# Attention and a gated convolution FFN on one core: P as the stationary operand, row sums from a column of ones, and an order of work written out

## The chip, the cores and the metric

The kernel runs on one core of one Trainium2 chip. The metric is the device time in microseconds (us). The kernel before has a median of 295.88 us over three runs (295.88 to 300.52).

## The reference

The core of what is computed, for 8 batches of 8 heads, 576 positions and 64 columns a head, in float32:

```python
scores = scale * np.matmul(q, k.transpose(0, 1, 3, 2))
cum = np.cumsum(np.log(np.clip(f, 0.0001, 1.0)), axis=-1)
decay = cum[:, :, :, None] - cum[:, :, None, :]
scores = np.where(causal, -1000000000.0, scores + decay)
attn = np.exp(scores - np.max(scores, axis=-1, keepdims=True))
attn = attn / (np.sum(attn, axis=-1, keepdims=True) + 1e-09)
x = np.matmul(attn, v)               # then heads side by side: 576 x 512 a batch
h = np.maximum(x @ w_in, 0.0)        # 576 x 1024
conv_out = sum(conv_w[k] * hp[:, k:k + S, :] for k in range(3))   # over positions, hp is h padded
out = (h * 1.0 / (1.0 + np.exp(-conv_out))) @ w_out
```

## The kernel before

Every batch has an attention part and an FFN part. Four heads make a group, `hb`, so there are 16 groups, two for each batch; two heads of a group are a pair, `i`.

Loading. `load_qk` (L199) fetches q and k of a group with transposing DMAs, seen as 16-bit halves of the float32 values: 128 rows, of which the odd ones hold the upper halves. The even rows carry the decay: `clamp` (L205, on VectorE) overwrites them for the first six groups, and `rows_of` (L220, L221) or, from the seventh group on, `fill` (L214, L215) bring constants and the cumulated logarithms from two images in DRAM, which `constants` and L289 to L291 write at the start. The first group adds the decay with two more matmuls (L323, L325). V comes in by `load_v` (L228, five DMAs a batch) and is cast to fp16 on GpSimd (`cast_v`, L234 and L236). Four q and k tiles go round.

Attention. The scores stand transposed: keys in partitions, queries along the columns (L320). `off_scores` does the blocks off the diagonal of one head in 1024 columns, `diag_scores` the four diagonal blocks of two heads, `tail_scores` the last 64 positions of four heads. ScalarE takes the exponentials from PSUM (L347, L357, L332). Diagonal and tail go through a float32 tile to GpSimd, which masks them (`diag_mask` L360, `tail_mask` L335). P then streams through TensorE twice (`sweep`, L381): `sums` with columns of ones as weights, the four pairs of a batch into one PSUM tile, and `pv` with V as weights, so that x comes out transposed. `recip` turns the sums round (L391) and inverts them (L392), `spread` spreads them over 64 partitions (L395), and `norm` multiplies (L404) into `xt`.

FFN. `ffn1` (L414) multiplies a 128-row tile of w_in with xt; `relu` (L418, ScalarE) halves the result; `conv` (L424, L426, VectorE) does the three taps; `tanh` (L429, ScalarE) and `gate` (L433, VectorE) make the gated value; `ffn2` (L440, L445, in the last batch L454, L457) multiplies with w_out; `evac` (L465, L467) copies from PSUM and `store` (L473, L476) writes. The weights come through GpSimd's DMA queue, which casts them (L500).

Order. `Plan.add` takes each piece of work with its engines, an estimated time, what it waits for, and a priority. `Plan.play` runs a list schedule over these when the program is built and emits the pieces in that order; at run time each engine follows its own queue in order. Four PSUM tiles of 1024 float32 columns (`ps`) are shared by all, with further limits (`sc`, `mm`, `pv`) on how many of them scores, ffn1 and P V may hold.

Of the kernel before, what the change touches and what calls it, by code (L numbers as in the profile page):

```python
# [9 lines left out]
FP32 = mybir.dt.float32  # L10
# [7 lines left out]

class Plan:


    ENGINES = ("PE", "ACT", "DVE", "POOL", "SP")

    def __init__(self, rooms):
        self.tasks = []
        self.rooms = rooms
        self.slot = {}

    def add(self, engines, after, key, fn, take=(), give=(), lag=0.2, dma=0.0, behind=()):
        after = [a for a in after if a is not None]  # L30
        behind = [a for a in behind if a is not None]
        self.tasks.append(dict(engines=engines, after=after, behind=behind, key=key, fn=fn, take=list(take),
                               give=list(give), lag=lag, dma=dma))
        return len(self.tasks) - 1

    def play(self, busy, dma_at, dma_ahead):
        tasks, rooms = self.tasks, self.rooms
        left = [len(t["after"]) + len(t["behind"]) for t in tasks]
        due, nxt = [[] for _ in tasks], [[] for _ in tasks]
        for k, t in enumerate(tasks):  # L40
            for a in t["after"]:
                due[a].append(k)
            for a in t["behind"]:
                nxt[a].append(k)
        free = {r: [(0.0, j) for j in range(n)] for r, n in rooms.items()}
        ready = {e: [] for e in self.ENGINES}
        busy = dict(busy)
        heap, order, started = [], [], set()
        dma_free, now = dma_at, 0.0

        def open_(k):
            for e in tasks[k]["engines"]:
                heapq.heappush(ready[e], (tasks[k]["key"], k))

        for k in range(len(tasks)):
            if not left[k]:
                open_(k)
        for e in self.ENGINES:
            heapq.heappush(heap, (busy[e], -1, ""))
        while len(started) < len(tasks):  # L60
            if not heap:
                raise RuntimeError("the plan is stuck")
            now = heap[0][0]
            while heap and heap[0][0] <= now:
                _, k, what = heapq.heappop(heap)
                if what == "give":
                    for r, taker in tasks[k]["give"]:
                        free[r].append((now, self.slot[taker, r]))
                elif what == "done":
                    for d in due[k]:  # L70
                        left[d] -= 1
                        if not left[d]:
                            open_(d)
            for e in self.ENGINES:
                if busy[e] > now:
                    continue
                kept = []
                while ready[e]:
                    key, k = heapq.heappop(ready[e])
                    if k in started:  # L80
                        continue
                    t = tasks[k]
                    if any(not free[r] for r in t["take"]):
                        kept.append((key, k))
                        continue
                    if t["dma"] and dma_free > now + dma_ahead:
                        kept.append((key, k))
                        heapq.heappush(heap, (dma_free - dma_ahead, -1, ""))
                        continue
                    for r in t["take"]:  # L90
                        free[r].sort()
                        self.slot[k, r] = free[r].pop(0)[1]
                    started.add(k)
                    for d in nxt[k]:
                        left[d] -= 1
                        if not left[d]:
                            open_(d)
                    order.append((now, k, e))
                    end = now + t["engines"][e]
                    busy[e] = end  # L100
                    heapq.heappush(heap, (end, -1, ""))
                    if t["dma"]:
                        dma_free = max(dma_free, now) + t["dma"]
                        end = max(end, dma_free)
                    if t["give"]:
                        heapq.heappush(heap, (end + 0.1, k, "give"))
                    heapq.heappush(heap, (end + t["lag"], k, "done"))
                    break
                for x in kept:
                    heapq.heappush(ready[e], x)  # L110
        return order, now
# [3 lines left out]
def kernel(  # L115
# [15 lines left out]
    NKB = 5  # L131
# [10 lines left out]
    RING, NP, NPT, NVA, NVF, NHT, NU, NOB = 4, 6, 4, 4, 2, 4, 3, 3  # L142
    NCL = 6
    AB = 256
# [4 lines left out]
    dpool = ctx.enter_context(tc.tile_pool(name="dram", bufs=1, space=bass.MemoryType.DRAM))  # L149
    psum = ctx.enter_context(tc.tile_pool(name="psum", bufs=1, space=bass.MemoryType.PSUM))  # L150

    image = dpool.tile([4, 2, BH, S], BF16, name="image")
    blank = dpool.tile([60, 2 * HS], BF16, name="blank")
    ident = cpool.tile([128, 128], FP32, name="ident")
# [4 lines left out]
    cwrow = cpool.tile([3, D_FF], FP32, name="cwrow")  # L159
    kc = cpool.tile([128, S], BF16, name="kc")  # L160
    one1 = cpool.tile([128, 1], FP32, name="one1")
    lim = cpool.tile([128, 4], FP32, name="lim")
    lit = cpool.tile([128, 5], FP32, name="lit")
    lii = cpool.tile([128, 3], I32, name="lii")
    hix = cpool.tile([128, 4], I32, name="hix")
    hfx = cpool.tile([128, 4], FP32, name="hfx")
    sel_k = cpool.tile([128, 4], BF16, name="sel_k")
    sel_q = cpool.tile([128, 4, 128], BF16, name="sel_q")
    ones_h = cpool.tile([128, 4, 64], FP16, name="ones_h")
# [4 lines left out]
    vf_t = [cpool.tile([128, H, NKB, 64], FP32, name=f"vf{t}") for t in range(NVF)]  # L174
    va_t = [cpool.tile([128, HH, NKB, 64], FP16, name=f"va{t}") for t in range(NVA)]
    pp_t = [cpool.tile([128, 3072], FP16, name=f"pp{t}") for t in range(NP)]
    pt_t = [cpool.tile([128, HH * SL], FP16, name=f"pt{t}") for t in range(NPT)]
    pd_t = [cpool.tile([128, 1024], FP32, name=f"pd{t}") for t in range(2)]
    p3_t = [cpool.tile([128, HH * SL], FP32, name=f"p3{t}") for t in range(2)]
    st_t = [cpool.tile([128, S], FP32, name=f"st{t}") for t in range(1)]  # L180
    rt_t = [cpool.tile([128, 18, 4], FP32, name=f"rt{t}") for t in range(2)]
    rb_t = [cpool.tile([128, S], FP32, name=f"rb{t}") for t in range(2)]
    xt_t = [cpool.tile([128, NCC, S], FP16, name=f"xt{t}") for t in range(2)]
    ht_t = [cpool.tile([128, S + 2], FP16, name=f"ht{t}") for t in range(NHT)]
    u_t = [cpool.tile([128, S], FP32, name=f"u{t}") for t in range(NU)]
    hg_t = [cpool.tile([128, NFF, S], FP16, name=f"hg{t}") for t in range(2)]
# [3 lines left out]
    fsb, cum = rb_t[0], rb_t[1]  # L190

    plan = Plan({"ps": 4, "sc": 2, "mm": 2, "pv": 2, "p": NP, "pt": NPT, "pd": 2, "p3": 2, "st": 1, "rt": 2, "rb": 2, "xt": 2, "ht": NHT,
                 "u": NU, "hg": 2, "ob": NOB, "va": NVA, "vf": NVF, "qk": RING})
    slot = plan.slot

# [7 lines left out]
    def clamp(hb, p, side, eng):  # L203
        t = (stq_t, stk_t)[side][hb % RING].bitcast(U16)[:, 2 * p * S:2 * (p + 1) * S]
        eng.tensor_scalar(t, t, lim[:, 2 * side:2 * side + 1], lim[:, 2 * side + 1:2 * side + 2],  # L205
                          op0=ALU.mult, op1=ALU.add)

    def even_rows(hb, first, n, c0, c1):
        t, width = qk_t[hb % RING], 2 * HS + 64
        return bass.AP(tensor=t.tensor, offset=int(t.offset) + first * width + c0, ap=[[2 * width, n], [1, c1 - c0]])  # L210

    def fill(hb):
        c = slice(hb * HH, (hb + 1) * HH)
        nc.sync.dma_start(even_rows(hb, 8, 60, 0, 2 * HS), blank)  # L214
        nc.sync.dma_start(even_rows(hb, 0, 4, 0, 2 * HS).rearrange("j (a x) -> j a x", a=2),  # L215
                          image[:, :, c, :].rearrange("j a h s -> j a (h s)"))

    def rows_of(hb):
        c = slice(hb * HH, (hb + 1) * HH)
        nc.sync.dma_start(even_rows(hb, 0, 1, 0, HS), image[0:1, 0, c, :].rearrange("j h s -> j (h s)"))  # L220
        nc.sync.dma_start(even_rows(hb, 2, 2, HS, 2 * HS), image[1:3, 1, c, :].rearrange("j h s -> j (h s)"))  # L221

    def load_v(b, t_load):
        vf = vf_t[slot[t_load, "vf"]]
        base = int(v.offset) + b * H * S * D
        for kb in range(NKB):
            n = 128 if kb < NKB - 1 else SL
            nc.sync.dma_start(vf[0:n, :, kb, :],  # L228
                              bass.AP(tensor=v.tensor, offset=base + kb * 128 * D, ap=[[D, n], [S * D, H], [1, D]]))
# [465 lines left out]
```

## Time and profile before

The profiled execution has a span of 293.2 us from first to last instruction, on the slowest (and only) core; what lies between it and the median of the runs, 2.7 us, is around the span.

| | busy us | share | instructions |
|---|---|---|---|
| TensorE matmul (PE) | 245.6 | 84% | 2832 |
| TensorE weight load (PEld) | 170.8 | 58% | 2832 |
| VectorE (DVE) | 238.9 | 81% | 322 |
| ScalarE (ACT) | 198.1 | 68% | 266 |
| GpSimd (POOL) | 96.2 | 33% | 133 |

The granted TensorE clock is 0.967 of full speed on average. DMA moves 47.7 MB in 125,683 packets. The first ffn1 matmul (L414) starts at 50.4 us, those of the later batches at 80.4, 114.7, 142.0, 173.2, 202.5, 231.8 and 256.7.

In profile lines, a group reads: line, engine, operation, output<-input, partitions by columns, type, count, busy us and the mean of one in ns. PE is TensorE, DVE VectorE, ACT ScalarE, POOL GpSimd, SP the queue that issues most DMAs. In a timeline the first two numbers are start and length in us. A busy time of PE counts each matmul until its modelled end, so it holds the drain of the pipeline as well as the columns that stream.

### The profile page before, as it was taken

Reading aid. Unit: us, or ns where it says so; the run is one execution under the profiler, and the core shown is the slowest. Engines: PE = TensorE matmul, PEld = TensorE weight load, DVE = VectorE, ACT = ScalarE, POOL = GpSimd, SP = SyncE. Lnnn points to the kernel's source line nnn. Section 1 sums busy time; section 2 is a strip of 40 time slices with the busy share of each in tenths; the row PEclk is TensorE's granted clock in tenths of the full one; section 3 lists DMA queues with packets and bytes.
Section 4 is the critical chain, followed back from the end, with each engine's and each line's share of the span. In section 5 each row is a group of like instructions: output and inputs, shape, how many; then the busy total and the mean of one; then the engine's idle time right before and its main releaser. Section 6 shows DMA issues by size and latency. Waiting matters only on the chain.

```text
span 293.2 us, 6856 instructions
## 1 busy us (share of the span) xinstructions
PE 245.6 (84%) x2832; PEld 170.8 (58%) x2832; DVE 238.9 (81%) x322; ACT 198.1 (68%) x266; POOL 96.2 (33%) x133
## 2 busy tenths in 40 slices
PE   0099539598789799999998999999999999969990
PEld 0078327376655577577755875687568757845630
DVE  4852308979999888997987899889988998899661
ACT  1228626487666998886877878977897798436631
POOL 8625907227340326306256261126112221000000
PEclk9999859979999999999999999999999999979998
DMA  8997999999998999999999999999322002100304
GB/s 164 215 246 127 165 182 188 173 191 191 218 191 127 293 218 169 238 246 268 177 211 227 254 205 198 211 296 178 80 77 80 11 2 104 62 0 32 132 0 162
DMA packets 125683, 47.71 MB, mean 163 GB/s; under 512 B 117470, under 2 KB 120542, under 8 KB 124992
## 3 DMA queue, kind: packets, MB, share of 16 engines
q1 hardware_dynamic: 118852, 43.73, 72.0%
q0 software_dynamic: 6640, 3.25, 8.0%
q8 instruction: 22, 0.36, 0.5%
q10 hardware_dynamic: 160, 0.30, 0.4%
q14 instruction: 9, 0.07, 0.1%
HBM read 19.91 MB, written 10.58 MB: 104 GB/s over the span
## 4 chain that ended last, share of the span: by engine, by line
PE 43%; DVE 24%; ACT 7%; issue 4%; DMA 2%; ACTq 0%; DVEq 0%
PE ps L440 14%; PE ps L414 11%; PE ps L381 8%; DVE u L426 6%; DVE hg L433 5%; PE ps L320 5%; DVE u L424 5%; DVE xt L404 3%; PE ps L454 3%; ACT pp L347 2%; ACT pd L357 2%; DVE rb L395 2%; DMA qk<-image 2%; ACT hg L429 2%; PE ps L445 1%
## 5 line engine op out<-in xcount | busy, mean ns | idle before, releaser
L320 PE MATMUL ps<-qk 128*128 128x128 bf16 (+3 forms) x576 | 63.7, 248 | 30.2 <-DVE qk L205 14.5
L414 PE MATMUL ps<-xt,w_in_f 128*128 128x288 f16 x512 | 74.1, 293 | 4.8 <-DVE xt L404 3.1
L347 ACT ACTIVATE pp<-ps 128x1024 f16<-128x1024 f32 x64 | 64.7, 1027 | 12.2 <-PE ps L320 9.8
L429 ACT ACTIVATE hg<-u,cw 128x576 f16<-128x576 f32 x64 | 49.4, 778 | 24.8 <-DVE u L426 24.5
L320 PEld LDWEIGHTS <-qk 128*128 128x128 bf16 x576 | 39.4, 101 | 42.8 <-issue 15.2
L414 PEld LDWEIGHTS <-w_in_f 128*128 128x128 f16 x512 | 49.9, 100 | 23.9 <-issue 7.3
L360 POOL TENSOR_SCALAR_AFFINE_SELECT pp<-pd 128x1024 f16<-128x1024 f32 x32 | 38.7, 1209 | 73.7 <-ACT pd L357 73.7
L433 DVE SCALAR_TENSOR_TENSOR hg<-hg,ht 128x576 f16<-128x576 f16 x64 | 52.9, 834 | 10.1 <-ACT hg L429 9.9
L424 DVE SCALAR_TENSOR_TENSOR u<-ht,cwt 128x576 f32<-128x576 f16 x64 | 56.4, 894 | 5.9 <-ACT ht L418 5.9
L426 DVE SCALAR_TENSOR_TENSOR u<-ht,cwt,u 128x576 f32<-128x576 f16 x64 | 60.1, 949 | 0.7
L418 ACT ACTIVATE ht<-ps 128x576 f16<-128x576 f32 x64 | 41.4, 657 | 18.9 <-PE ps L414 14.1
L440 PE MATMUL ps<-w_out_f,hg 128*128 128x512 f16 x224 | 51.4, 379 | 2.7 <-ACT pd L357 1.2
L440 PEld LDWEIGHTS <-hg 128*128 128x128 f16 x224 | 21.7, 98 | 26.5 <-issue 2.3
L357 ACT ACTIVATE pd<-ps 128x1024 f32<-128x1024 f32 x32 | 32.8, 1025 | 5.9 <-PE ps L325 2.5
L381 PE MATMUL ps<-pp,ones_h 128*64 128x128 f16 (+3 forms) x576 | 26.3, 242 | 1.5 <-ACT pp L347 0.9
L381 PEld LDWEIGHTS <-ones_h 128*64 128x64 f16 x640 | 23.0, 112 | 6.3 <-issue 4.6
L381 PE MATMUL ps<-pp,va 128*64 128x128 f16 (+3 forms) x576 | 24.8, 239 | 1.7 <-DVE xt L404 1.2
L335 POOL TENSOR_SCALAR_AFFINE_SELECT pt<-p 128x256 f16<-128x256 f32 x16 | 10.3, 641 | 48.7 <-ACT p L332 48.7
L234 POOL CAST va<-vf 128x1024 f16<-128x1024 f32 x16 | 17.8, 1113 | 24.1 <-DMA vf<-in_v_dram 18.1
L381 PEld LDWEIGHTS <-va 128*64 128x64 f16 x640 | 22.4, 110 | 5.6 <-issue 4.1
L395 DVE STREAM_TRANSPOSE rb<-rt 128x576 f32<-128x576 f32 x32 | 22.7, 745 | 0.0
L404 DVE TENSOR_TENSOR xt<-ps,rb 128x576 f16<-128x576 f32 x32 | 22.0, 725 | 0.0
(75 smaller groups left out, 167.6 us busy)
## 6 DMA issues: line engine op xcount, KB each, us to landing
vf<-in_v_dram SPq DMA_DIRECT2D x32, 256.0 KB, 5.6
out_dram<-ob SPq DMA_DIRECT2D x16, 512.0 KB, 2.8
qk<-blank SPq DMA_DIRECT2D x10, 540.0 KB, 5.3
vf<-in_v_dram SPq DMA_DIRECT2D x8, 128.0 KB, 5.1
w_in_f<-in_moe_w_in_dram POOLq DMA_DIRECT2D x4, 256.0 KB, 6.0
w_out_f<-in_moe_w_out_dram POOLq DMA_DIRECT2D x4, 256.0 KB, 7.7
out_dram<-ob SPq DMA_DIRECT2D x16, 64.0 KB, 3.8
blank<-qk POOLq DMA_DIRECT2D x1, 540.0 KB, 4.7
```

What stands on the lines that cost most here:

```text
L320: nc.tensor.matmul(o, tk[:, h * S + k0:h * S + k0 + 128], tq[:, h * S + q0:h * S + q0 + n], start=True, stop=hb > 0)
L347: nc.scalar.activation(pp_t[slot[t_dg, "p"]][:, 1024 * s:1024 * (s + 1)], ps_t[slot[t_sc, "ps"]], AF.Exp, scale=SCALE)
L357: nc.scalar.activation(pd_t[slot[me, "pd"]], ps_t[slot[t_dg, "ps"]], AF.Exp, scale=SCALE)
L360: nc.gpsimd.affine_select(pp_t[slot[t_dg, "p"]][:, 2048:3072].rearrange("p (m j) -> p m j", j=128), pd_t[slot[t_ex, "pd"]].rearrange("p (m ...
L381: nc.tensor.matmul(ps[64 * s:64 * (s + 1), AB + q0:AB + q0 + n], left_of(s, h, m), p, start=first and x in (0, 3), stop=last and x in (2, ...
L414: nc.tensor.matmul(ps[:, MB + 288 * a:MB + 288 * (a + 1)], w_in_f16[:, cc, 128 * ff:128 * (ff + 1)], xt[:, cc, 288 * a:288 * (a + 1)], sta ...
L418: nc.scalar.activation(ht_t[slot[t_m1, "ht"]][:, 1:1 + S], ps_t[slot[t_m1, "ps"]][:, MB:MB + S], AF.Relu, scale=0.5)
L424: nc.vector.scalar_tensor_tensor(u, ht[:, 0:S], cwt[:, ff, 0:1], ht[:, 1:1 + S], op0=ALU.mult, op1=ALU.add)
L426: nc.vector.scalar_tensor_tensor(u, ht[:, 2:2 + S], cwt[:, ff, 1:2], u, op0=ALU.mult, op1=ALU.add)
L429: nc.scalar.activation(hg_t[slot[t_g0, "hg"]][:, ff, :], u_t[slot[t_u, "u"]], AF.Tanh, scale=cw[:, ff, 1:2])
L433: nc.vector.scalar_tensor_tensor(hv, hv, 1.0, ht_t[slot[t_m1, "ht"]][:, 1:1 + S], op0=ALU.add, op1=ALU.mult)
L440: nc.tensor.matmul(o, hg[:, ff, 128 * c:128 * (c + 1)], w_out_f16[:, ff, :], start=(ff == 0), stop=(ff == NFF - 1))
```

## The change

Scores, exponentials, FFN matmuls and their numbers stay. What differs:

- P V: a block of P (128 keys by 128 queries) is the stationary operand, and 65 columns of V move: 64 of a head and one of ones, so that each row sum stands beside its row. x comes out with positions in partitions; `norm` inverts the sums and multiplies, and `turn` transposes x on TensorE into `xt`'s layout, with `turned` copying it on VectorE or ScalarE. `sums`, `recip` and `spread` go.
- Masks of the first eight groups: a matmul puts -1e30 into PSUM above the diagonal before the scores are added, and the exponential goes straight to P in fp16. The other eight groups keep GpSimd's masks.
- Convolution of eight of the 64 tiles (even tiles of batches 0 and 1): three matmuls with diagonal matrices, and tanh reads PSUM.
- Weights: loaded as float32 through SP in eight pieces into the tiles for outputs, and cast by GpSimd, VectorE or ScalarE.
- The two DRAM images go; constants come from an SBUF tile `zc` (`fill`), the rows from `kc`. Clamps serve four groups instead of six, one for each side of a group.
- Order: `play` emits the pieces in the order of the string `ORDER`, which also names the engine of the evacuations, the xt copies and the weight casts. One more `ht` and one more `u` buffer; the limits `sc`, `mm` and `pv` go.

The core of the diff, new functions included:

```diff
+ORDER = """
+q1.1 cl1.1 q3.1 cw q3.0 q2.0 q1.0 cl0.0 sd0 ed0 q2.1 cl0.1 sd1 cl2.0 cwt so0.0 eo0.0 cl1.0 so1.0 eo1.0 v0.0 rw1 ed1
+so0.1 eo0.1 so1.1 eo1.1 v0.3 st0 et0 sd2 so2.1 ed2 so2.0 eo2.0 st1 et1 sd3 so3.1 tw0 ed3 eo3.1 tw2 so3.0 eo3.0 v0.2
+cl2.1 v0.1 rw2 cl3.1 v0.4 va0.0 eo2.1 v1.0 v1.1 va1.0 va1.1 pv0.0 n0.0 va0.1 wi0 cl3.0 sd4 ed4 wi1 wic1@POOL v1.2 sd5
...
+o7.1.2 a7.7 o7.1.3 o7.1.4 o7.1.5 g7.7 o7.1.6 o7.1.7 s5.0 o7.0.4 o7.0.5 o7.0.6 o7.0.7 e6.2@ACT s6.2 o7.2.0 o7.2.1
+o7.2.2 o7.2.3 o7.2.4 o7.2.5 o7.2.6 o7.2.7 e7.1@ACT s7.1 e7.0@ACT s7.0 e7.2@ACT s7.2
+"""
...
+    MASK_PE = (0, 1, 2, 3, 4, 5, 6, 7)
+    CONV_PE = ((0, 0), (0, 2), (0, 4), (0, 6), (1, 0), (1, 2), (1, 4), (1, 6))
...
+    def masked(o, n, j):
+        nc.tensor.matmul(o, ident, mask[:, 0:j].unsqueeze(1).broadcast_to((128, n, j)), start=True, stop=False)
...
+    def pv(hb, u):
+        ps, va = ps_of(f"pv{hb}.{u}"), va_t[slot[f"va{hb}.0", "va"]]
+        for j, n in enumerate(((0, 1), (2, 3), (4,))[u]):
+            for h in range(HH):
+                o = ps[:, 512 * j + (D + 1) * h:512 * j + (D + 1) * (h + 1)]
+                for m in range(n + 1):
+                    nc.tensor.matmul(o, block(hb, h, m, n), va[:, h, m, 0:D + 1], start=(m == 0), stop=(m == n))
+
+    def norm(hb, u):
+        ps, rc, xm = ps_of(f"pv{hb}.{u}"), rc_t[slot[f"n{hb}.{u}", "rc"]], xm_t[slot[f"n{hb}.0", "xm"]]
...
+        nc.vector.reciprocal(r, got[:, :, :, D])
+        nc.vector.tensor_tensor(xm[:, 2 * u:2 * u + nj, :].rearrange("p j (h d) -> p j h d", d=D), got[:, :, :, 0:D],
+                                r.unsqueeze(3).broadcast_to((128, nj, HH, D)), op=ALU.mult)
+
+    def turn(hb):
+        ps, xm = ps_of(f"t{hb}").bitcast(FP16), xm_t[slot[f"n{hb}.0", "xm"]]
+        for n in range(NKB):
+            c = 128 * n if n < 4 else S - 128
+            for cc in range(2):
+                nc.tensor.transpose(ps[:, 1024 * cc + c:1024 * cc + c + 128], xm[:, n, 128 * cc:128 * (cc + 1)], ident)
...
+    def conv_pe(b, ff):
+        ps, ht = ps_of(f"k{b}.{ff}"), ht_of(b, ff)
+        for x in range(3):
+            for a in range(2):
+                nc.tensor.matmul(ps[:, MB + 288 * a:MB + 288 * (a + 1)], taps[:, ff, x, :],
+                                 ht[:, x + 288 * a:x + 288 * (a + 1)], start=(x == 0), stop=(x == 2))
...
+    def fill(hb):
+        for first, n, side in ((0, 63, 0), (2, 62, 1)):
+            src = zc[first:first + n, side:side + 1, :].broadcast_to((n, HH, S))
+            nc.sync.dma_start(even_rows(hb, first, n, side * HS, (side + 1) * HS).rearrange("p (h s) -> p h s", s=S), src)
+
+    def rows_of(hb):
+        c = hb * HH
+        nc.sync.dma_start(even_rows(hb, 63, 1, 0, HS), kc[c:c + HH, :])
+        for j in range(2):
+            nc.sync.dma_start(even_rows(hb, j, 1, HS, 2 * HS), kc[BH * j + c:BH * j + c + HH, :])
```

In `ORDER`, q and k loads are `q<group>.<side>`, V loads `v`, clamps `cl`, rows `rw` and `fi`, scores `sd`, `so`, `st`, their exponentials `ed`, `eo`, `et`, GpSimd's masks `md`, `mt`, P V `pv`, its norm `n`, transposes `t` and `tx`, weights `wi`, `wo` with casts `wic`, `woc`; then ffn1 `f`, relu `r`, convolution `c`, `d` or on TensorE `k`, tanh `a`, gate `g`, ffn2 `o`, evacuation `e`, store `s`.

## The prediction

> **What bounds the kernel now.** I read the page's engine totals first, then the busy time by stretch, then the chain of waits, then groups and timeline for prices.
>
> ```profile
> PE 245.6 (84%) x2832; PEld 170.8 (58%) x2832; DVE 238.9 (81%) x322; ACT 198.1 (68%) x266; POOL 96.2 (33%) x133
> ...
> PE 43%; DVE 24%; ACT 7%; issue 4%; DMA 2%; ACTq 0%; DVEq 0%
> ```
>
> TensorE (PE) and VectorE (DVE) are nearly equal in load, and no engine alone fills the span. So I asked for the busy time by stretch: until the first ffn1 matmul (50.4 us), from there to the first ffn1 matmul of the last batch (256.7), to the end, and for two steady batches in between.
>
> ```profile
> 0.00:50.40 50.40, 27.31 (x349) 21.00 (x349) 23.21 (x46) 21.85 (x24) 28.42 (x63) 0.90 1.02 182
> 50.40:256.70 206.30, 190.64 (x2327) 135.64 (x2325) 190.14 (x243) 160.31 (x219) 67.79 (x71) 0.99 0.87 175
> 256.70:293.20 36.50, 27.66 (x160) 14.19 (x159) 25.56 (x35) 15.94 (x23) 0.00 (x0) 0.93 0.18 65
> ...
> 173.20:202.50 29.30, 28.32 (x345) 20.01 (x345) 27.46 (x36) 24.26 (x34) 9.25 (x11) 1.00 1.07 226
> 202.50:231.80 29.30, 28.33 (x345) 20.03 (x345) 27.47 (x36) 24.26 (x34) 7.42 (x8) 1.00 0.26 76
> ```
>
> Columns after the length are PE, PEld, DVE, ACT, POOL busy, granted clock, DMA share, GB/s. A steady batch takes 29.3 us with PE 28.3 and DVE 27.5 busy: two engines hand the bound to each other. The chain of waits shows the handover, PE work and then the normalisation on DVE alone:
>
> ```profile
> 188.12 0.98 PE ps L414 x8
> 189.09 0.44 PE ps L320 x4
> 189.53 2.21 PE ps L381 x60
> ...
> 194.43 0.70 DVE st L391
> 195.16 0.60 DVE rt L392
> 195.76 1.44 DVE hg L433
> 197.20 0.75 DVE rb L395 x2
> ```
>
> A busy PE is not PE at its pace, since each matmul's span holds its drain. So I price matmuls start to start. The first score stage, after the clock has come up at 21.5 us, has single rows:
>
> ```profile
> 22.01 0.19 PE L320 MATMUL ps<-qk 128*128 128x64 bf16 x1
> 22.04 0.19 PE L323 MATMUL ps<-sel_k,kc 128*128 128x64 bf16 x1
> 22.07 0.19 PE L325 MATMUL ps<-kc,sel_q 128*128 128x64 bf16 x1
> ...
> 22.75 0.22 PE L320 MATMUL ps<-qk 128*128 128x128 bf16 x1
> 22.81 0.22 PE L323 MATMUL ps<-sel_k,kc 128*128 128x128 bf16 x1
> 22.86 0.22 PE L325 MATMUL ps<-kc,sel_q 128*128 128x128 bf16 x1
> ```
>
> 64 columns cost about 29 ns, 128 cost 56, each with a fresh 128x128 weight load in front. From the chain: ffn1 0.98 us per 8 (0.98 x 64 = 62.7), one sweep of L381 2.21/3 = 0.74 (64 sweeps, 47.2), ffn2 7.8 a batch (62.2), scores 2.76 per four heads (44.1, plus 5.5 for the first four heads' extra products). Paced PE work before is 222 us; in 50.4 to 256.7 it is 54.9 + 46.8 + 35.7 + 41.3 = 178.7, or 87% of the 206.3 us; in the two steady batches 54.0 of 58.6, 92%.
>
> **The change, part by part.** On PE: the 64 sweeps go, -47.2. P V becomes 960 pairs of a 128x128 load and a 65-column matmul. No row has 28 such pairs running; the nearest are the 64-column rows, 29 ns, so 30 ns is taken: 28.8. If nothing of the load were hidden, it would be the 100 ns that an LDWEIGHTS of L320 lasts: 96. The low end is 27 ns (the fastest gap of the rows above). 160 transposes at 128 columns: 56 ns, 9.0; between 56 and the same 100 ns load, 16. Mask products of the first eight groups of four heads: 32 of 512 columns at 0.216 (the chain's 1.73 per 8) and 8 of 256, 7.8. Convolution of eight tiles: 48 of 288 columns at 0.1225, 5.9. Net +4.3: PE stays at 226.6, a wash.
>
> The Trainium skill, page "TensorE: Matmul & The Clock Gate", section "Back-to-back issue gap", speaks against this change: it gives about 81 ns for a sustained stream of load-and-matmul pairs at 128 columns. The rows above give 56 ns for such pairs; by the page's figure the 960 pairs would take 78 us and the kernel, as an estimate, some 316.
>
> On DVE: spread, norm, st and rt go (rows L395 22.7, L404 22.0, L391 6.2, L392 4.8), 55.7. Eight of 64 convolutions leave, (56.4 + 60.1)/8 = 14.6. Clamps cover a third fewer elements of 16.1, 5.4. The clip of f (L282), 3.97 us beside POOL's 4.0 us memset of qk (L263), has no such memset now; L286 does a like size in 0.46, so 3.5. Sum removed 79.2. Added: 48 norm products from PSUM. L404 does 576 columns in 0.725 and the 1024-column copy (L467) takes 1.22, so 1.11 ns a column: 32 at 0.65 and 16 at 0.37, 26.7. Reciprocals of 4 or 8 columns, by the 8-column row 0.20: 9.8, by L392's 0.60 at most 28.9. Eight xt copies of 1152 columns, 1.37 each, 10.9; five more large evacuations and a small one 6.5; one weight cast 1.2; masks and identity 0.5. Sum added 55.6. DVE: 215.3 against 238.9. Beyond that, DVE suffers when POOL masks:
>
> ```profile
> 177.02 0.81 DVE L424 SCALAR_TENSOR_TENSOR u<-ht,cwt 128x576 f32<-128x576 f16 x1
> ...
> 178.42 1.64 DVE L426 SCALAR_TENSOR_TENSOR u<-ht,cwt,u 128x576 f32<-128x576 f16 x1
> ...
> 178.22 1.23 POOL L360 TENSOR_SCALAR_AFFINE_SELECT pp<-pd 128x1024 f16<-128x1024 f32 x1 [3.25 <-ACT pd L357]
> ```
>
> Half the POOL masks go; means above 0.81 (0.89 and 0.95, gate 0.83 against 0.75) make 20 us of such loss, so 0 to 10 more off DVE, 6 taken (POOL gets six weight casts of the size of L234, 1.1 us, in exchange). ACT: eight xt copies at 1.1 (between L465's 1.0 and one and an eighth of it), one cast, less five evacuations: 198 + 4.5.
>
> The queues: POOL's 15 DMA issues and the image and blank copies go. SP gets eight weight loads, 24 fills (L214 row 0.88 us) and 45 single rows (L220 0.36), 43 us of issuing in place of 20. The view of SP's waits has it waiting 63 us for evacuations at L473 alone, so this is covered in the steady part. It isn't at the start, where SP issues in order: four half loads until 7 us, six full transposes at 2.65 us each (rows of L199) until 23, the row copies of the second four heads behind their clamp at about 27, landing at 30 (that group's scores started at 27.4 before); while SP stands at them, V's loads wait behind, and POOL's V casts with them. The weight loads follow V at about 33 and are cast by 42, behind ACT's work. What then sets the first ffn1 is ACT's queue: seven exponentials from 16, the rest from 30 on, 15 at about 0.95 (mean 1.03, overlapping by a tenth), so 45 us, with the third and half the fourth group of heads already scored. It was 50.4.
>
> Sum: from first ffn1 to the last batch's, counted in the new order by the same paces, PE has 54.9 ffn1, 45.9 ffn2, 35.1 scores, 25.2 P V, 7.8 transposes, 4.5 masks, 5.8 convolutions, 179.2. DVE's part of this stretch is 215.3 - 6 less some 27 of head and 17 of tail, 165, so 87% of 190 us, where it was 94% in the steady batches. I take a PE efficiency of 94% (steady before 92, whole before 87): 190.6. The tail holds 24.3 us of PE; DVE's eight tiles of 2.14 take 17.1 after 1.6 of ffn1 and relu, then 3.0 of last ffn2, 1.4 evacuation, the 6.3 from the last store's issue to the end, some 2 of earlier gates: 32 against 36.5. 45 + 190.6 + 32 = 267.6, against the profiled 293.2; the median lies 2.7 above that span, so 270.3.
>
> **The rivals.** (1) Every P V pair pays its weight load. For: L381's loads last 110 ns and P is now always the loaded side, 60 pairs per group. Against: the 29 ns rows. At 100 ns the middle grows by 840 x 0.07/0.94 = 62.6 and the head by 4.2: 337 us. It decides from about 63 ns a pair on, where the time passes 302; at 56 ns it is 295, no change.
> (2) The fixed order doesn't meet the real delays: an engine waits at the head of its queue for work that is late while ready work stands behind, and PE stays at its old 87%. For: 33 takes of four PSUM tiles a batch, 30 before. Against: DVE's slack. 179.2/0.866 = 206.9, total 287.
> (3) The start gains nothing, as all loads pass through SP: first ffn1 at 50 to 54. 276 to 279; in the range.
>
> **How the numbers follow.** Forecast with (3) 0.64; better than 258 (98% efficiency, head 43, tail 30) 0.06; rival (2) 0.15, a third of it within 2%; rival (1) 0.15, of which 0.04 ends near 56 ns, within 2%, and 0.11 slower. Faster 0.64 + 0.06 + 0.10 = 0.80, same 0.05 + 0.04 = 0.09, slower 0.11; 2% is about what a measurement of this kernel tells from no change. The range goes from 258 to 288, just past rival (2).
>
> **What would show it.** Right: 65-column matmuls at 30 ns start to start; DVE busy 205 to 215; first ffn1 near 45; 190 us from there to the last batch's. Wrong: those matmuls 60 ns or more apart, a PE idle share as large as before with DVE well below 80%, or SP still issuing first loads when PE stands.

## The result, and the profile after

The changed kernel takes 331.69 us (median of four runs, 328.07 to 332.81), the kernel before, beside it on the same chip, 295.88 us: a ratio of 1.1217, with a 95% interval from 1.1117 to 1.1317. It is slower by 12%, where 270 us had been forecast. The profiled execution has a span of 329.4 us.

First the engine totals, the shares of the chain that ended last (by engine, then by line), and three groups (busy us, mean ns of one, idle before):

```profile
PE 255.7 (78%) x2760; PEld 181.6 (55%) x2760; DVE 207.6 (63%) x327; ACT 203.3 (62%) x269; POOL 70.7 (21%) x109
...
SPq 46%; PE 23%; DMA 20%; POOL 4%; DVE 2%; issue 2%; ACT 2%; ACTq 0%
SPq L195 15%; SPq L215 11%; PE ps L459 10%; DMA qk<-in_q_dram 9%; DMA qk<-kc 7%; SPq L217 7%; SPq L223 5%; PE ps L414 5%; SPq L211 5%; PE ps L308 4%; SPq L477 2%; PE ps L384 2%; DMA ob<-in_moe_w_in_dram 2%; POOL taps L435 2%; DMA vf<-in_v_dram 1%
...
L384 PE MATMUL ps<-va,pp 128*128 128x65 f16 x896 | 36.0, 197 | 0.5 <-ACT pp L349 0.2
...
L391 DVE RECIPROCAL rc<-ps 128x8 f32<-128x8 f32 (+1 forms) x48 | 9.3, 194 | 36.4 <-PE ps L384 35.7
...
L392 DVE TENSOR_TENSOR xm<-ps,rc 128x512 f16<-128x512 f32 (+1 forms) x48 | 28.9, 602 | 1.7
```

The loads of the engines are as forecast: DVE went from 238.9 to 207.6 us. What changed is who ends the wait. Before, PE and DVE held two thirds of the chain and SP none of the lines shown; now SP's issuing (SPq) and transfers (DMA) hold two thirds, 46% and 20%.

Next the busy time by stretch: to the first ffn1 matmul, from there to the last batch's, the tail; then two batches in the middle, a bad one and a good one.

```profile
0.00:46.50 46.50, 29.56 (x353) 22.57 (x354) 21.18 (x53) 21.08 (x23) 15.46 (x47) 0.96 1.00 197
46.50:300.10 253.60, 201.13 (x2235) 144.36 (x2233) 165.94 (x247) 165.03 (x222) 55.20 (x63) 0.91 0.66 146
300.10:329.40 29.30, 24.98 (x177) 14.63 (x175) 20.48 (x29) 17.19 (x26) 0.00 (x0) 0.96 0.34 121
109.00:167.60 58.60, 40.35 (x391) 26.69 (x390) 30.68 (x45) 30.39 (x40) 11.63 (x12) 0.88 0.57 133
167.60:192.90 25.30, 25.30 (x310) 18.53 (x309) 22.48 (x35) 22.88 (x31) 8.02 (x9) 1.00 0.86 190
```

Head 46.5 us (45 forecast) and tail 29.3 (32) are better than before. The middle, 253.6 us where 190.6 had been forecast, holds the whole loss. One of its batches takes 25.3 us with PE busy throughout; in another PE is idle for 31% (40.35 of 58.6) and DVE and ACT for nearly half, with the granted clock down to 0.88.

What PE and its weight loads waited for in the whole run (total us, times, longest), from the view of the waits of each:

```profile
PE ps L308 <- DMA qk<-kc: 42.7, 10, 8.3
...
PEld L308 <- DMA qk<-zc: 30.1, 6, 8.2
```

L308 is the score matmul. It waits for the rows of constants (`zc`) and of cumulated logarithms (`kc`) in q and k. One such wait in the chain (start, length, what):

```profile
78.06 0.70 SPq L211
...
78.81 3.37 SPq L215
...
82.23 1.49 SPq L217
...
83.77 6.49 DMA qk<-kc
90.26 0.09 issue
90.35 0.37 PE ps L308 x4
```

`fill` issues its second piece (L211) in 0.70 us. The next instruction, a copy of one row for each of four heads in one 4.5 KB DMA (L215), then takes 3.37 us to issue, and the first of two more (L217) 1.49; the second, whose issue begins at 83.77 us, lands 6.5 us after that. Only then do the scores of the group start. The view of the transfers for 76 to 91 us shows why, in 40 slices of 0.375 us (busy share of 16 DMA engines in tenths, and rate):

```profile
DMA  9959799765642111111111111111197899995006
GB/s 246 252 120 139 246 377 404 248 190 147 172 144 95 46 37 34 34 37 49 49 43 43 49 49 43 46 37 40 40 180 146 320 389 358 278 133 29 27 18 134
```

For 16 slices, 6 us, the share is a tenth and the rate 34 to 49 GB/s. The packet records of the trace say what runs there. They hold no engine's number, but the packets in flight at a time can be counted: two for the k-side fill, 62 rows of 4 x 1152 bytes, whose 248 packets of about 52 ns each take some 6.4 us; nine for the q-side fill, 63 rows. The kernel before fills a group with 60 rows. In its transfers from 83.5 to 92 us (slices of 0.21 us) the long run of nines is a transpose in 256-byte packets; the fill's 60 packets of 9216 bytes begin only from the thirteenth slice on, at 86.1 us:

```profile
DMA  3199999999309009849459056210000001003899
GB/s 47 35 113 287 290 289 289 290 290 289 63 7 477 0 0 173 304 173 434 173 173 520 0 109 152 65 43 0 0 0 0 0 0 43 0 0 88 204 181 73
```

Of these 60, 15 are in flight at a time from 87 to 88.5 us, and the last ends at 89.3: about 3 us for 540 KB, against 6.4 us for the 62 rows' 279 KB. The Trainium skill, page "DMA: Bandwidth & Descriptors", section "Why a DMA increments its semaphore by 16 and not by 1", has the rule: a copy is spread over the largest number of engines, at most 16, that divides the slowest dimension above 1 of both its sides. The packets in flight agree: 15 for 60 rows, 9 for 63, 2 for 62. Below, packets in flight stand for engines.

The P V matmuls, start to start, at about 41 us (the same columns; xN counts matmuls drawn together):

```profile
40.19 1.56 PE L384 MATMUL ps<-va,pp 128*128 128x65 f16 x44
41.59 0.19 PE L384 MATMUL ps<-va,pt 128*128 128x65 f16 x1
41.62 0.29 PE L384 MATMUL ps<-va,pp 128*128 128x65 f16 x4
41.75 0.19 PE L384 MATMUL ps<-va,pt 128*128 128x65 f16 x1
```

44 take 41.59 - 40.19 = 1.40 us, 32 ns each, with a fresh 128x128 load of P in front of every one.

### The profile page after: what moved, and what is told of

It is laid out like the page before. It is cut to its first block, busy times and chain, and to the rows that moved or that the text cites. A ratio compares the mean times of both kernels' runs of the same rounds, so it can differ in the third digit from the quotient of the medians.

```text
span 329.4 us, 6715 instructions
## 1 busy us (share of the span) xinstructions
PE 255.7 (78%) x2760; PEld 181.6 (55%) x2760; DVE 207.6 (63%) x327; ACT 203.3 (62%) x269; POOL 70.7 (21%) x109
## 4 chain that ended last, share of the span: by engine, by line
SPq 46%; PE 23%; DMA 20%; POOL 4%; DVE 2%; issue 2%; ACT 2%; ACTq 0%
SPq L195 15%; SPq L215 11%; PE ps L459 10%; DMA qk<-in_q_dram 9%; DMA qk<-kc 7%; SPq L217 7%; SPq L223 5%; PE ps L414 5%; SPq L211 5%; PE ps L308 4%; SPq L477 2%; PE ps L384 2%; DMA ob<-in_moe_w_in_dram 2%; POOL taps L435 2%; DMA vf<-in_v_dram 1%
## 5 line engine op out<-in xcount | busy, mean ns | idle before, releaser
L308 PE MATMUL ps<-qk 128*128 128x128 bf16 (+2 forms) x576 | 72.7, 262 | 59.8 <-DMA qk<-kc 42.7
L308 PEld LDWEIGHTS <-qk 128*128 128x128 bf16 x576 | 45.6, 108 | 82.3 <-DMA qk<-zc 30.1
L366 ACT ACTIVATE pp<-ps 128x1024 f16<-128x1024 f32 x64 | 63.8, 1024 | 14.3 <-PE ps L308 11.0
L459 PE MATMUL ps<-w_out_f,hg 128*128 128x512 f16 x256 | 64.5, 402 | 0.8 <-DVE xm L392 0.8
L429 DVE SCALAR_TENSOR_TENSOR u<-ht,cwt 128x576 f32<-128x576 f16 x56 | 46.6, 836 | 10.0 <-ACT ht L424 9.7
L431 DVE SCALAR_TENSOR_TENSOR u<-ht,cwt,u 128x576 f32<-128x576 f16 x56 | 46.2, 836 | 1.3
L384 PE MATMUL ps<-va,pp 128*128 128x65 f16 x896 | 36.0, 197 | 0.5 <-ACT pp L349 0.2
L384 PEld LDWEIGHTS <-pp 128*128 128x128 f16 x896 | 34.3, 100 | 2.5 <-ACT pp L349 0.5
L349 ACT ACTIVATE pp<-ps 128x1024 f16<-128x1024 f32 x16 | 16.3, 1028 | 30.5 <-PE ps L308 19.4
L349 ACT ACTIVATE pd<-ps 128x1024 f32<-128x1024 f32 x16 | 16.3, 1024 | 24.4 <-PE ps L308 24.0
L352 POOL TENSOR_SCALAR_AFFINE_SELECT pp<-pd 128x1024 f16<-128x1024 f32 x16 | 18.4, 1158 | 57.3 <-ACT pd L349 57.3
L392 DVE TENSOR_TENSOR xm<-ps,rc 128x512 f16<-128x512 f32 (+1 forms) x48 | 28.9, 602 | 1.7
```

The source lines that it names most:

```text
L308: nc.tensor.matmul(o, tk[:, h * S + k0:h * S + k0 + 128], tq[:, h * S + q0:h * S + q0 + n], start=first, stop=last and hb > 0)
L366: nc.scalar.activation(pair(i)[:, s, 512:1536], ps_of(f"so{i}.{s}"), AF.Exp, scale=SCALE)
L384: nc.tensor.matmul(o, block(hb, h, m, n), va[:, h, m, 0:D + 1], start=(m == 0), stop=(m == n))
L429: nc.vector.scalar_tensor_tensor(u, ht[:, 0:S], cwt[:, ff, 0:1], ht[:, 1:1 + S], op0=ALU.mult, op1=ALU.add)
L431: nc.vector.scalar_tensor_tensor(u, ht[:, 2:2 + S], cwt[:, ff, 1:2], u, op0=ALU.mult, op1=ALU.add)
L459: nc.tensor.matmul(ps[:, 512 * (c % 2):512 * (c % 2 + 1)], hg_of(b, ff)[:, 128 * c:128 * (c + 1)], w_out_f16[:, ff, :], **kw)
```

## The experiments

"Before" ran beside each, and ratios are to it. The theory: the 62-row fill, alone on two engines, delays the rows behind it and with them the scores. Rivals: SP's many issues in order, the places of work in `ORDER`, or the masks and convolutions that went to PE.

**Both sides cut to 48 + 15 and 48 + 14 rows.**

```diff
-        for first, n, side in ((0, 63, 0), (2, 62, 1)):
+        for first, n, side in ((0, 48, 0), (48, 15, 0), (2, 48, 1), (50, 14, 1)):
```

> Both fills of a group are cut in two (48 + 15 rows, 48 + 14 rows), same bytes, two more issues a group. Theory A, few engines: the 62-row fill runs on two DMA engines only (two packets in flight for 6 us in the trace), and the row copies behind it wait in the same rings; cut at 48 it runs on 16 and 14. Then L215's issue falls from 3.4 to about 0.6 us, L217's from 1.3 to 0.6, no stretch with two 1152-byte packets in flight is left, and the time falls to 270 to 297 us (the lower end is the sum of the prediction). Rival B, the row copies themselves are slow to issue (four runs out of four partitions), and SP has too many issues: L215 stays at 3.4 us, 24 more issues of 0.8 us make it slower, about 345 us.

Measured 281.7 us, ratio 0.9554 [0.949, 0.9619]: 50 us off, with 24 DMA issues more. The issue of L215 (ns: least, median, most) in the kernel after, and then here:

```profile
L215 SPq DMA_DIRECT2D qk<-kc x15: 634/3374/3572, 25.7 to 272.2; - x15
```

```profile
L215 SPq DMA_DIRECT2D qk<-kc x15: 625/657/917, 25.5 to 232.1; - x15
```

**Only the k side cut.**

```diff
+        for first, n, side in ((0, 63, 0), (2, 48, 1), (50, 14, 1)):
```

> Only the k side's 62-row fill is cut (48 + 14); the q side's 63 rows stay. Theory A: 63 rows run on nine engines, 28 packets each of 52 ns, 1.5 us, which is no obstacle, so nearly the whole gain of the even fill is here, 270 to 297 us, and one issue a group less. If both sides matter alike, half the gain, about 310 us. Rival B: 12 more issues, about 340 us.

Measured 280.94 us, ratio 0.9511 [0.9423, 0.9599]: the 62 rows are all of it, as far as these runs can tell; cutting the 63 rows too, in the run before, gained nothing more. The wait of the scores, 42.7 us in the kernel after, is nearly gone:

```profile
PE ps L308 <- DMA qk<-kc: 4.8, 3, 2.3
```

This version serves as the base below. Its totals and chain, and its three longest middle stretches:

```profile
PE 243.0 (88%) x2760; PEld 174.7 (63%) x2760; DVE 211.7 (76%) x327; ACT 202.3 (73%) x269; POOL 73.7 (27%) x109
...
PE 39%; SPq 24%; DVE 13%; DMA 12%; ACT 5%; issue 4%; POOL 1%; DVEq 0%; POOLq 0%
```

```profile
95.40:140.10 44.70, 38.25 (x392) 25.79 (x391) 31.27 (x45) 30.10 (x39) 11.32 (x12) 0.92 0.83 179
...
165.40:193.80 28.40, 27.71 (x342) 20.34 (x341) 27.45 (x40) 23.07 (x31) 7.34 (x7) 1.00 1.03 203
193.80:223.10 29.30, 27.65 (x331) 20.03 (x330) 26.39 (x40) 27.02 (x36) 9.69 (x10) 1.00 0.98 189
```

**The k side made worse: 61 rows, and 1.**

```diff
+        for first, n, side in ((0, 63, 0), (2, 61, 1), (63, 1, 1)):
```

> The cost doubled: 62 rows cut as 61 + 1, so that 61 rows, a prime number, go on one engine: 244 packets of 52 ns, 12.7 us a group where it is 6.4 now. Theory A: up to 6.3 us more for each of 12 groups on SP's chain, so 360 to 405 us, and L215's issue about 9 us. Rival B: 12 more issues of 0.7 us, about 340 us.

Measured 383.49 us, ratio 1.3012 [1.2911, 1.3114]. One packet of the 61 rows is in flight at a time, and the wait of the scores grows with it; the second line is the issue of the fills' pieces (ns: least, median, most):

```profile
PE ps L308 <- DMA qk<-kc: 73.1, 11, 9.9
...
L211 SPq DMA_DIRECT2D qk<-zc x36: 670/899/9377, 55.0 to 319.0; - x36
```

One detail was missed: L215 stays at a median of 0.60 us. The long issue fell on the instruction right behind the slow piece, which is now the 1-row piece of L211 (longest 9.4 us).

**The kernel after with its fills uncut, on GpSimd's queue.**

```diff
-            nc.sync.dma_start(even_rows(hb, first, n, side * HS, (side + 1) * HS)...
+            nc.gpsimd.dma_start(even_rows(hb, first, n, side * HS, (side + 1) * HS)...
```

> The fills go through GpSimd's queue, uncut; the rows stay on SP. Theory A in the form that the rows stand behind the fill's packets in SP's rings: L215's issue falls to 0.6 us, and 290 to 315 us, because the fill itself may still land late. Rival B: L215 stays at 3.4 us and only the two fill issues leave SP, 12 x 1.6 = 19 us, 312 us.

Measured 356.42 us, ratio 1.2006 [1.1837, 1.2174], so the expected time was wrong. L215 does issue in 0.66 us, so the rows no longer stand behind the fills; but now the fills themselves come late (DMA issues: count, KB each, median us from issue to landing):

```profile
qk<-zc POOLq DMA_DIRECT2D x12, 283.5 KB, 6.0
qk<-zc POOLq DMA_DIRECT2D x12, 279.0 KB, 13.7
```

63 rows land in 6.0 us, 62 in 13.7, with nine and two packets in flight as on SP. So SP's blocked issue is one form of the cost; the slow landing is its root, and another queue doesn't remove it. Not all of the time need be the landing: GpSimd stands idle for 42.8 us in all before its fills, with its casts and masks behind them in order, and the two were not separated.

**The cause put into the kernel before: its 60-row fill cut to 58 + 2.**

```diff
-        nc.sync.dma_start(even_rows(hb, 8, 60, 0, 2 * HS), blank)
+        nc.sync.dma_start(even_rows(hb, 8, 58, 0, 2 * HS), blank[0:58, :])
+        nc.sync.dma_start(even_rows(hb, 124, 2, 0, 2 * HS), blank[58:60, :])
```

> The kernel before with its 60-row fill cut as 58 + 2 rows, same bytes, one more issue for each of ten groups. Theory of few engines: 60 rows run on 15 engines (15 packets in flight in its trace), 58 = 2 x 29 rows on two, 29 packets of 0.53 us, 15.4 us where it was 2.1, and the row copies behind them wait too: some 10 us for those of the ten fills that aren't issued early, 310 to 350 us. Rival, only the count of issues matters: 10 x 0.85 us on a queue with room, 294 to 298 us.

Measured 355.72 us, ratio 1.2151 [1.2078, 1.2225], a little above what was expected. Apart from one more issue a fill nothing else differs. Two packets of a fill are in flight, for 10 to 12 us, and the wait is of the kind of the kernel after: for the rows, which here come from the row image. First the kernel before, then this run (lines shifted by one):

```profile
PE ps L320 <- DMA qk<-image: 11.7, 2, 8.3
```

```profile
PE ps L321 <- DMA qk<-image: 42.9, 5, 13.6
```

**Masks back on GpSimd, and convolutions back on VectorE, each alone on the base.**

```diff
+    MASK_PE = ()        # the one run; md0, mt0 and their like come into the order
+    CONV_PE = ()        # the other; k0.0 and its like become c0.0 d0.0 in the order
```

> On top of e2_k_side, the masks of the first eight groups go back to GpSimd, so one part of the change is undone. The prediction's prices: PE loses 7.8 us, GpSimd gains 24 masks, VectorE loses about 6 us to them. If PE bounds the first half: 273 to 277. If VectorE's and GpSimd's share decides: 282 to 288. No change: 279 to 283.

> On top of e2_k_side, the eight convolutions on PE go back to VectorE and the twelve tap matrices on GpSimd are left out. Prices: PE loses 5.9 us, VectorE gains 14.6, GpSimd loses 9. If PE bounds the first two stretches (it is 22.3 of 25.4 and 24.0 of 24.6 us busy there): 275 to 279. If VectorE does: 283 to 289.

Measured 284.96 us, ratio 0.9684 [0.9608, 0.976], and 286.63 us, ratio 0.975 [0.9687, 0.9814]. Against the base's 280.94, masks on PE gain 4.0 us and the eight convolutions 5.7 (about 5 and 7 by the ratios); neither interval meets the base's, the masks' by a hair (0.9608 against 0.9599). PE's busy time falls by 7.5 and 3.5 us without them and the kernel gets no faster, so neither was the loss.

**What keeps the base 11 us above the forecast.** The third stretch takes 44.7 us for 34.0 us of paced PE work (matmuls counted at their start-to-start prices). Of the 10.7 us between, PE is idle for 6.5, and the granted clock of 0.92 is worth some 3.6 more (0.08 of 44.7, an estimate). The base's chain in it:

```profile
90.78 0.34 SPq L195
...
94.46 2.13 SPq L195
...
98.34 2.17 SPq L211
...
118.49 1.07 SPq L477
...
119.61 0.58 SPq L477
120.24 4.09 DMA vf<-in_v_dram
124.40 0.08 issue
124.48 1.04 POOL va L230
125.57 0.82 PE ps L384 x12
```

SP issues for 29 us without a pause (transposes, fills, rows, V, a store); V lands after it, is cast, and P V goes on. PE idles 6.5 us in the stretch, so a cure of this chain can win that and what the clock regains, no more. Five runs tried to shorten it.

```diff
# V loads on GpSimd's queue
-        nc.sync.dma_start(vf[0:n, :, kb, :],
+        nc.gpsimd.dma_start(vf[0:n, :, kb, :],
```

> On top of the k side's cut fill (e2_k_side, 280.9 us), V's 40 loads go through GpSimd's queue, where the cast that needs them stands anyway. Theory: once the fills are spread, SP's own issuing is what is late, above all from 91 to 122 us of that run, where SP issues without a pause and the chain of waits runs through it; 40 issues of 0.6 us leave, so the third stretch between first ffn1 matmuls falls from 44.7 us towards its 34.0 us of PE work, and the total to 268 to 274. Rival: the DMA engines themselves are full there (share about 1.0), so nothing is won, 278 to 283. Second rival: GpSimd's in-order queue makes V late or its descriptor work slows VectorE, over 285.

Measured 305.88 us (298.15 to 308.18; the runs scatter too widely for a ratio). Even the fastest lies 17 us above the base. V now stands in GpSimd's order behind masks that wait for ScalarE. In the profiled run, one of 304.69 us, the first ffn1 starts at 47.9 us in place of 45.4 and the third stretch takes 52.4. That is the time of the expectation's second rival; which of its two reasons acts was not separated.

```diff
# order: the five loads of batch 3 and of batch 4 change places
-... t4 v4.0 r1.7 ... v4.1 ... v4.4 ... v3.0 ... v3.4 ... v3.3 ... v3.2 ... v3.1 ... v4.3 ... v4.2
+... t4 v3.0 r1.7 ... v3.1 ... v3.2 ... v3.3 ... v3.4 ... v4.0 ... v4.1 ... v4.2 ... v4.3 ... v4.4
```

> On top of e2_k_side, only the written order changes: the ten positions in which V of batches 3 and 4 is loaded stay, but all five pieces of batch 3 come first, where three pieces of batch 4 stood before batch 3's first. In e2_k_side the third stretch between first ffn1 matmuls takes 44.7 us for 34.0 us of PE work, and its chain runs over SP without a pause from 91 to 120 us into V's landing at 124 and the P V of batch 3. Theory, the order keeps V late: the pieces come up to 11 us earlier, the stretch falls to 36 to 40, the total by 4 to 8 to 273 to 277 us. Rival, SP's issuing of transposes and fills is late in itself, so that scores stand still anyway: 279 to 283.

```diff
# the same order, and the k side as 60 + 2 rows
+        for first, n, side in ((0, 63, 0), (2, 60, 1), (62, 2, 1)):
```

> The same, and the k side's fill cut as 60 + 2 rows in place of 48 + 14: 60 rows on 15 engines, 16 packets each, then 8 packets on two. Fewer packets stand before the rows in the first engines; the 14-row piece took 1.3 to 2.3 us to issue. Theory: the second piece's issue falls to about 0.6 us, 12 x 1 us less on SP, half of it on the chain, 3 to 6 us under the other kernel of this call. Rival: the wait for room moves to the row copies, the same time within 2 us.

Measured 281.79 us, ratio 0.9494 [0.945, 0.9538], and 282.63 us, ratio 0.9525 [0.9477, 0.9573]: no gain. V comes earlier, and the store at the end of SP's run is what PE then waits for, by way of its buffer and a VectorE evacuation.

```diff
# groups 6 and 7 clamped on VectorE in place of filled
-            if hb < NCL:
+            if hb in CLAMPED:        # (0, 1, 2, 3, 6, 7); fi6, fi7 become cl6, cl7 and rw6, rw7
```

> The version with the k side cut (281 us), with the constants of groups 6 and 7 written by the DVE clamp that groups 0 to 3 have, in place of six fill pieces on SP. In that version's chain SP issues without a pause from 90.8 to 120 us, and the six pieces are 3.8 + 3.7 us of it; then V lands (4.1 us), POOL casts it and PE goes on; the third stretch (first ffn1 to first ffn1) is 44.7 us for 34 us of paced PE work. Theory: SP's issuing in order is what is left of the miss: the stretch becomes 37 to 39 us and the kernel 274 to 277. Rival: the stretch is set by PE and DVE work and the handovers between them, and V would only have been the last of several: four clamps of 0.87 us are added to DVE there, the stretch stays at 43 to 46, the kernel at 279 to 284.

```diff
# stores on ScalarE's queue
-                nc.sync.dma_start(outf[...
+                nc.scalar.dma_start(outf[...
```

> The version with the k side cut (281 us), with all stores issued from ScalarE's queue in place of SP's, at the same places of the order. One store stands in SP's run of issues before 120 us (1.07 + 0.58 us), and later ones make SP wait for evacuations that DVE does. Theory: SP's order is the bound, so what stands behind the stores comes earlier: 276 to 279. Rival: the stores behind SP's run cost nothing that PE waits for, 280 to 283; and if ScalarE stands at stores whose evacuation DVE has not done, its exponentials come late and it takes 283 to 290.

The clamps: 276.74 us, ratio 0.9384 [0.9307, 0.946], the fastest here and by its median within what the theory expected, but its interval overlaps that of the base (0.9511). The engines' shares of its chain:

```profile
PE 42%; SPq 18%; DVE 18%; DMA 10%; ACT 5%; issue 5%; POOL 1%; DVEq 0%
```

SP's share falls from 24 to 18%, DVE's rises from 13 to 18. The stretch itself shrinks to 40.2 us, less than expected, and the one before it grows from 24.6 to 28.3, so the fourth batch's ffn1 starts only 1.1 us earlier (139.0 against 140.1). Between theory and rival, then: with SP relieved, more of the chain lies on PE and DVE. The stores: 287.03 us, ratio 0.9758 [0.9672, 0.9845], slower than the base. Two later stretches grow to 31.5 and 33.7 us (from 25.3 and 28.4), as the rival's second part said; ScalarE waits 3.7 us there for `ob` buffers that stores still read, which the base doesn't show. Where the rest goes was not followed.

## Why the prediction was wrong, by its steps

**The step that failed is the queue term.** "24 fills (L214 row 0.88 us) and 45 single rows (L220 0.36), 43 us of issuing in place of 20", "covered in the steady part". The fills do issue in 0.82 us. But that row was the issue of a 60-row fill on 15 engines, and nothing in it prices 62 rows: the landing (some 6 us on two engines), and what is behind it. The first row copy then issues in 3.37 us, the other two in 1.34 each (medians), and the last lands some 6.5 us after its issue begins:

```profile
L211 SPq DMA_DIRECT2D qk<-zc x24: 694/817/959, 55.6 to 271.4; - x24
...
L217 SPq DMA_DIRECT2D qk<-kc x30: 573/1342/1721, 26.5 to 277.0; - x30
```

Summed over the trace, fills, rows and weight loads take 107 us to issue where 43 had been counted: 20 for the fills, 80 for the rows, 7 for the weights. In the base it is still 73: its 36 pieces of fills take 38, and a row copy takes 0.58 to 0.76 us (medians), not 0.36. Nor was the issuing covered: SP still waits 36.9 us for evacuations at the stores (L474, the L473 of before) and yet holds 46% of the chain, since a queue that works in order can't use a wait at one place for issues that stand at another.

From the kernel after to the base with the k side cut, the middle goes from 253.6 to 202.4 us: 51.2 us over 12 fills, 4.3 us each. Of these, 38.5 us are idle PE (52.5 against 14.0), and 12.7 are longer PE busy time for the same matmuls (201.1 against 188.4), which goes with a granted clock of 0.91 against 0.98. Cutting these rows alone turned 12% slower into 5% faster, and cutting the fill of the kernel before alone made that one 22% slower, so this cause is shown. The term had no upper end at all; "SP still issuing first loads when PE stands" named SP only for the start.

**The head and the tail held in their times, less so in their paths.** First ffn1 starts at 46.5 us (45), in the base at 45.4, so rival (3), 50 to 54, fell; but ScalarE, whose queue was to set it, stands idle for 3.7 of the 15 us before. The tail takes 29.3 us (32). Its chain is PE's matmuls alone until 324.1 us, then ScalarE's evacuation and the store; VectorE's 17.1 us, the largest term of that sum, aren't in it. That the sum came near is luck in part.

**The middle at 94%.** Where no fill is late it was even better: the steady batch of 25.3 us is PE all the way, in the kernel after and in the base. The base's whole middle is 202.4 us for 179.2 us of paced work, 89%, nearer to rival (2)'s 87% than to the forecast. Without the third stretch it is 157.7 us for 145.2, 92%. So the base's 280.94 us against 270.3 comes apart as head +0.4, middle +11.8, tail -2.6, and 1.0 between the profiled span and the median (the profiled run, 278.89 us, is the fastest of the four). When SP lost two groups' fills the median fell by 4.2 us, within the noise, and the fourth batch's ffn1 came 1.1 us earlier. How much of the excess is SP's issuing and how much rival (2), ready work behind late work, was not separated; it stays open.

**Rival (1), the weight loads, fell.** From one P V pair to the next it is 32 ns in the median and 29 at the least, 90% within 35, against a turning point of 63; 960 at 29 to 32 ns are 28 to 31 us. The transposes, pairs at 128 columns, keep 55 to 56 ns. The Trainium skill's figure, page "TensorE: Matmul & The Clock Gate", section "Back-to-back issue gap", about 81 ns for a sustained stream of pairs at 128 columns, doesn't show in these runs, nor the 78 us for P V that the prediction estimated by it.

**VectorE's account held as a sum, 207.6 us for 205 to 215.** Norm products take 0.69 and 0.42 us (0.65 and 0.37), reciprocals 0.19 (0.20). Two terms were mis-sized and nearly cancel, which is luck: an xt copy on VectorE takes 0.76 us, not 1.37 (the row it was scaled from reads float32, this one fp16); the one weight cast takes 4.95 us, not 1.2, beside GpSimd's casts.

## What to carry to other kernels

A DMA had three prices here: its issue, its landing, and the wait that it put on the small transfers behind it in its queue. Read the row count of every new or resized copy as a divisor question first: two rows more (62 for 60) took a fill from 15 engines to 2, and that was the difference between a 5% gain and a 12% loss; cutting it into pieces that divide well gave all of that back. Engine totals don't show it; the chain's shares (SPq and DMA) and the busy share of the DMA engines do.

## What the runs showed of the hardware that was not expected

- An issue's length can belong to the transfer in front of it: 0.60 to 0.66 us became 3.37 behind a 62-row fill, and up to 9.4 behind one of 61 rows, while the slow fill's own issue stayed at 0.8. That the queue of the two engines had no room is my reading; no record shows it.
- GpSimd's queue spreads no better: two packets in flight for 62 rows, which landed after 13.7 us there, and nine for 63, after 6.0.
- In these stretches the granted clock is lower where PE waits: 0.88 in the stretch of 58.6 us, 0.92 in the base's 44.7, 1.00 in the 25.3 us where PE never stands. So a wait cost more than its own length: 12.7 us of longer busy time beside 38.5 us of idle PE.
